# Decode attention and gated MLP in one kernel: q projection for both batch rows at once, turn sums on VectorE, the last part of W_up loaded apart, output in four column tiles

## The chip, the cores and the metric

One core of one Trainium2 chip. Times are device microseconds (us) of one execution, medians of several. The profile's span leaves out about 1.8 us that the measured time includes (661.62 us measured, span 659.8 us in the profiled run of before).

## The reference

Two batch rows, one new token each. A layer norm, attention over a cache of 8192 positions with 32 heads of 128, an output projection with residual, then a second layer norm and a gated MLP with residual. Everything is bf16.

```python
# B=2, Sq=1, D=512, 32 heads, Sk=8192, Dh=128, F=1376
xn = layernorm(x)
q = (xn @ wq) -> (B, 32, 1, 128)
p = softmax(q @ k_cache^T * 128**-0.5)          # k_cache, v_cache: (2, 32, 8192, 128)
h = x + (p @ v_cache) @ wo
g = layernorm(h) @ W_gate; u = layernorm(h) @ W_up
out = h + (relu(g) * u) @ W_down
```

The two caches hold 2 x 2 x 32 x 8192 x 128 x 2 bytes = 268 MB; with the weights, 281 MB have to be read.

## The kernel before

The heads are taken in 16 groups: 4 heads of one batch row each, 8.4 MB of K and 8.4 MB of V per group. K is multiplied by q and added up on VectorE, the exponential is taken on ScalarE, and V is weighted on TensorE. SBUF holds two K tiles and one V tile, so the loads form one long queue on SyncE.

```python
# q, before: one batch row at a time, 32 columns, 64 matmuls
for b in range(B):
    for g in range(0, NQ, QP):
        qps = ps_mm.tile([P, QP, Dh], f32, tag="mm", name="qps")
        for h in range(G):
            for c in range(KC):
                nc.tensor.matmul(out=qps[h*Q:(h+1)*Q], lhsT=xnb[:, c, b, :],
                                 rhs=wq_v[:, c, g:g+QP, h, :], ...)
        nc.scalar.activation(out=qrep[:, b, g:g+QP, :], in_=qps, func=ACT.Copy)
...
def blocks_of(o):            # four "turns" of o, scaled apart on ScalarE, summed by four matmuls
    osb = opool.tile([P, TG, Dh], f32, tag="row", name="osb")
    for t in range(TG):
        nc.scalar.activation(out=osb[:, t, :], in_=o[:, t*Dh:(t+1)*Dh], func=ACT.Copy,
                             scale=turn_of[:, t:t+1])
    return osb
...
for n in range(N - 1):
    scores(n, ...)           # VectorE, then ScalarE's exponentials
    load_k(n + 2)
    weighted_v(n)            # TensorE; at the end of a pair of groups: blocks_of and matmuls
    load_v(n + 1)
...
# the order of the last loads: wo, V of group 15 in four cuts, W_gate, W_up, W_down (three blocks
# and a remainder wd_l)
def y_rows(lhsT, rhs, first=False, last=False):
    m = lhsT.shape[1]
    for e in range(2):       # the output's two halves side by side in two column tiles of TensorE
        nc.tensor.matmul(out=y_ps[e*Q:e*Q+m], lhsT=lhsT, rhs=rhs[:, e*HD:(e+1)*HD], ...)
...
y_row = opool.tile([2 * Q, HD], bf16, tag="row")
nc.vector.tensor_copy(y_row, y_ps[0:2 * Q])
for e, eng in ((0, nc.sync), (1, nc.scalar)):
    eng.dma_start(out=out.rearrange("b s (h n) -> h (b s) n", n=HD)[e],
                  in_=y_row[e * Q:e * Q + B, :])
```

Here P = 128, Q = 32, KC = 4, HD = 256, B = 2. Each row of `o` counts in only one of its four blocks of 128 columns, its "turn"; the mask `turn_of` (0 or 1) picks that block. A column tile is a group of 32 output partitions that has matmuls of its own.

The softmax here doesn't subtract the row's maximum and nothing guards it: scores larger than these inputs give would overflow.

## Time and profile before

Median 661.66 us of three runs (661.63 to 661.9).

| | us | share of the span |
|---|---|---|
| VectorE busy | 592.1 | 90% |
| TensorE busy | 126.5 | 19% |
| ScalarE busy | 64.0 | 10% |
| packets on the load queue, as share of 16 engines | | 98.8% |

The page's busy line, its DMA line by slices of a 40th of the span, the table of DMA queues, and the shares of the chain that ended last, of the kernel before:

```profile
PE 126.5 (19%) x1390; PEld 64.0 (10%) x1391; DVE 592.1 (90%) x180; ACT 64.0 (10%) x175; POOL 2.5 (0%) x8
DMA  9999999999999999999999999999999999999996
q1 hardware_dynamic: 7124, 281.06, 98.8%
q8 instruction: 11, 0.18, 0.1%
DMA 77%; PE 15%; another core or an unknown queue 8%; issue 0%; DVE 0%; ACT 0%; ACTq 0%
```

VectorE's 90% looks like the limit, but the DMA engines are fuller: nine tenths or more in every slice but the last. The windows view of before shows it by stage; its last two columns are the DMA share and GB/s:

```profile
12.00:652.00 640.00, 120.83 (x1316) 59.73 (x1316) 587.30 (x150) 60.74 (x170) 0.00 (x0) 0.59 1.00 432
652.00:654.00 2.00, 1.52 (x43) 1.53 (x44) 0.05 (x1) 0.00 (x0) 0.00 (x0) 0.50 0.65 233
654.00:656.00 2.00, 1.67 (x20) 1.00 (x19) 0.24 (x2) 0.00 (x0) 0.00 (x0) 0.50 0.09 33
```

So for 640 us nothing is to be won unless fewer bytes are moved or the loads themselves run faster than this, and the end consists of what has to follow the stream. That end, from the timeline of before (start, duration, engine, line, operation, tiles):

```profile
652.48 1.74 PE L505 MATMUL up_ps<-hd,W 128*128 128x2 bf16 x44 [1.11 <-DMA W<-in_B_W_up_dram]
654.26 0.24 DVE L523 TENSOR_TENSOR act<-gate,up_ps 96x2 bf16<-96x2 f32 x2 [2.22 <-PE up_ps L505]
654.55 2.30 PE L456 MATMUL y_ps<-W,act 128*2 128x256 bf16 x20 [0.33 <-DVE act L523]
656.64 0.42 PE L456 MATMUL y_ps<-wd_l,act 96*2 96x256 bf16 x2
657.11 0.42 DVE L530 CAST y_row<-y_ps 64x256 bf16<-64x256 f32 x1 [2.61 <-PE y_ps L456]
657.55 0.32 SPq L532 DMA_DIRECT2D out_dram<-y_row  x1
657.55 0.26 ACTq L532 DMA_DIRECT2D out_dram<-y_row  x1
```

W_up's landing releases the up matmuls, they release the activation, that the y matmuls, then the cast and the two stores, issued at 657.55; the span ends 2.3 us later.

### The profile page before, as it was taken

The numbers are of one execution on the slowest core, as the hardware profiler recorded it, in microseconds if no ns is written. First come the engines' busy times: TensorE is split into PE (matmuls) and PEld (weight loads), VectorE is DVE, ScalarE is ACT, GpSimd is POOL, SyncE is SP. The second block draws the span as 40 slices with busy tenths as digits, with TensorE's granted clock in tenths as the row PEclk, the third lists the DMA queues.
The fourth block names the chain that finished last, engine by engine and source line by source line (L and its number), as shares of the span: only waits on it lengthen the run. The fifth ranks groups of instructions, "written<-read, shape, count | busy, mean of one in ns | idle before, by whom it ended". The sixth has DMA issues, their size and how long they took to land.

```text
span 659.8 us, 3322 instructions
## 1 busy us (share of the span) xinstructions
PE 126.5 (19%) x1390; PEld 64.0 (10%) x1391; DVE 592.1 (90%) x180; ACT 64.0 (10%) x175; POOL 2.5 (0%) x8
## 2 busy tenths in 40 slices
PE   2100302103030210404013030401203030030456
PEld 1000101001010000202002010100001010010225
DVE  2699999999998989989899998989899898999942
ACT  2101010010101010010102001010000101011020
POOL 1000000000000000000000000000000000000000
PEclk9755755757575565755656575565657555575766
DMA  9999999999999999999999999999999999999996
GB/s 382 445 445 445 402 425 441 445 445 434 402 441 437 445 434 413 433 437 438 441 433 418 441 425 445 434 429 429 425 441 438 441 421 437 421 442 437 402 413 248
DMA packets 7156, 281.28 MB, mean 426 GB/s; under 512 B 762, under 2 KB 1380, under 8 KB 2148
## 3 DMA queue, kind: packets, MB, share of 16 engines
q1 hardware_dynamic: 7124, 281.06, 98.8%
q8 instruction: 11, 0.18, 0.1%
q14 instruction: 5, 0.04, 0.0%
q10 hardware_dynamic: 16, 0.01, 0.0%
HBM read 281.06 MB, written 0.00 MB: 426 GB/s over the span
## 4 chain that ended last, share of the span: by engine, by line
DMA 77%; PE 15%; another core or an unknown queue 8%; issue 0%; DVE 0%; ACT 0%; ACTq 0%
DMA v<-in_A_v_cache_dram 70%; PE o L250 13%; DMA W<-in_B_W_up_dram 4%; DMA wq_sb<-in_A_wq_dram 2%; DMA W<-in_A_x_dram 1%; PE qps L175 1%; PE y_ps L456 0%; PE up_ps L505 0%; DVE y_row L530 0%; DVE act L523 0%; ACT osb L260 0%; ACTq L260 0%
## 5 line engine op out<-in xcount | busy, mean ns | idle before, releaser
L215 DVE TENSOR_TENSOR k<-k,qrep 128x32768 bf16<-128x32768 bf16 (+1 forms) x17 | 275.7, 16218 | 33.1 <-DMA k<-in_A_k_cache_dram 33.1
L221 DVE TENSOR_TENSOR k<-k 128x16384 bf16<-128x16384 bf16 (+3 forms) x68 | 266.8, 3923 | 2.3
L250 PE MATMUL o<-v,pm 128*32 128x512 bf16 x1016 | 90.9, 535 | 500.1 <-DMA v<-in_A_v_cache_dram 500.1
L250 PEld LDWEIGHTS <-pm 128*32 128x32 bf16 x1016 | 38.6, 129 | 550.3 <-issue 381.7
L227 ACT ACTIVATE pm<-sc 32x256 bf16<-32x256 f32 x64 | 47.2, 737 | 346.6 <-DVE sc L224 345.3
L224 DVE TENSOR_REDUCE sc<-k 128x256 f32<-128x2048 bf16 (+1 forms) x17 | 36.7, 2160 | 2.0 <-DVE k L221 0.5
L260 ACT ACTIVATE osb<-o,turn_of 128x128 f32<-128x128 f32 x36 | 10.3, 368 | 210.5 <-PE o L250 210.5
L227 ACT ACTIVATION_READ_ACCUMULATOR pm<-sc 32x1 f32 x64 | 15.0, 234 | 0.0
L296 PE MATMUL rep<-osb,spread 128*64 128x128 f32 (+1 forms) x64 | 9.9, 297 | 3.9 <-ACT osb L260 3.9
L462 DVE TENSOR_SCALAR o_sum<-o,turn_of 128x128 f32<-128x128 f32 x1 | 0.3, 350 | 10.8 <-PE o L250 10.8
L296 PEld LDWEIGHTS rep<-osb,spread 128*64 128x64 f32 (+1 forms) x64 | 7.3, 161 | 8.7 <-ACT osb L260 7.8
L175 PE MATMUL qps<-wq_sb,xnb 128*32 128x512 bf16 x64 | 5.7, 532 | 4.8 <-DMA wq_sb<-in_A_wq_dram 4.8
L442 PE MATMUL ar_ps<-W,oc 128*2 128x512 bf16 x28 | 3.2, 626 | 11.4 <-DVE oc L347 11.4
L152 DVE COPY xc<-x_ps 128x8 f32<-128x8 f32 x1 | 0.2, 167 | 4.9 <-PE x_ps L149 4.9
L505 PEld LDWEIGHTS <-W 128*128 128x128 bf16 (+1 forms) x88 | 3.4, 122 | 1.4 <-DMA W<-in_B_W_up_dram 1.2
L175 PEld LDWEIGHTS <-xnb 128*32 128x32 bf16 x64 | 2.8, 123 | 7.3 <-issue 5.8
L181 ACT ACTIVATE qrep<-qps 128x512 bf16<-128x512 f32 x4 | 2.4, 597 | 6.5 <-PE qps L175 6.5
L530 DVE CAST y_row<-y_ps 64x256 bf16<-64x256 f32 x1 | 0.4, 417 | 2.6 <-PE y_ps L456 2.6
L456 PE MATMUL y_ps<-W,act 128*2 128x256 bf16 x20 | 2.3, 415 | 0.3 <-DVE act L523 0.3
L523 DVE TENSOR_TENSOR act<-gate,up_ps 96x2 bf16<-96x2 f32 (+1 forms) x2 | 0.2, 160 | 2.2 <-PE up_ps L505 2.2
L320 PE MATMUL zb<-zm,same 128*128 128x4 f32 (+2 forms) x12 | 2.0, 283 | 0.3 <-ACT ol_f L287 0.3
L442 PEld LDWEIGHTS <-oc 128*2 128x2 bf16 x28 | 0.8, 113 | 12.9 <-DVE oc L347 11.5
(91 smaller groups left out, 47.6 us busy)
## 6 DMA issues: line engine op xcount, KB each, us to landing
k<-in_A_k_cache_dram SPq DMA_DIRECT2D x2, 4096.0 KB, 30.8
wq_sb<-in_A_wq_dram SPq DMA_DIRECT2D x1, 4096.0 KB, 12.3
v<-in_A_v_cache_dram SPq DMA_DIRECT2D x1, 4096.0 KB, 15.8
v<-in_A_v_cache_dram SPq DMA_DIRECT2D x1, 3072.0 KB, 22.8
W<-in_A_wo_dram SPq DMA_DIRECT2D x1, 2048.0 KB
W<-in_B_W_gate_dram SPq DMA_DIRECT2D x1, 1376.0 KB, 26.9
W<-in_B_W_up_dram SPq DMA_DIRECT2D x1, 1376.0 KB
W<-in_A_wo_dram SPq DMA_DIRECT2D x1, 1024.0 KB, 28.7
```

Of the source, the lines that this page charges most:

```text
L175: nc.tensor.matmul(out=qps[h * Q:(h + 1) * Q], lhsT=xnb[:, c, b, :], rhs=wq_v[:, c, g:g + QP, h, :], start=(c == 0), stop=(c == KC - 1),)
L181: nc.scalar.activation(out=qrep[:, b, g:g + QP, :], in_=qps, func=ACT.Copy)
L215: nc.vector.tensor_tensor(out=kp, in0=kp, in1=_view(qrep[:, b, i, :], 0, [[0, hi - lo], [1, Dh]]), op=ALU.mult)
L221: nc.vector.tensor_tensor(out=kp[:, :, 0:half], in0=kp[:, :, 0:half], in1=kp[:, :, half:width], op=ALU.add)
L224: nc.vector.tensor_reduce(out=sc[:, lo:hi], in_=kp[:, :, 0:8], axis=AXIS.X, op=ALU.add)
L227: nc.scalar.activation(out=p_of[ps, :, :, h], in_=sc[ps, :].rearrange("p (g t) -> p g t", t=TG), func=ACT.Exp, accum_out=(zm[ps, b, i:i + ...
L250: nc.tensor.matmul(out=o[g:g + W2], lhsT=_view(pm, (0 if lane else R) + t // TG * W2, [[1, W2]]), rhs=vt[:, t:t + TG, :].rearrange("p t d ...
L260: nc.scalar.activation(out=osb[:, t, :], in_=o[:, t * Dh:(t + 1) * Dh], func=ACT.Copy, scale=turn_of[:, t:t + 1])
L296: nc.tensor.matmul(out=reps[where][at:at + m, max(k - 1, 0), :], lhsT=spread[n_of].rearrange("k u h m -> k (u h m)"), rhs=osb[:, t, :], st ...
L442: nc.tensor.matmul(out=ar_ps[g:g + B], lhsT=oc[:, k, :], rhs=wo_sb[:, k, :], start=False, stop=(k + P // Q >= NK), skip_group_check=True)
L456: nc.tensor.matmul(out=y_ps[e * Q:e * Q + m], lhsT=lhsT, rhs=rhs[:, e * HD:(e + 1) * HD], start=first, stop=last, skip_group_check=True)
L505: nc.tensor.matmul(out=ps[0:w, fc, :], lhsT=lhsT, rhs=hd[:, c, :], start=(c == 0 and fc == 0), stop=(c == KC - 1), skip_group_check=True)
```

## The change

Its intent: halve the matmuls of the q projection; replace four scalings and four f32 matmuls per pair of groups by four VectorE operations and one matmul, and do them after the next scores; let most of the up matmuls start before the last quarter of W_up; run the y matmuls four at a time. The diff, cut to its core:

```diff
-    for b in range(B):
-        for g in range(0, NQ, QP):
+    for g in range(0, NQ, QP):
+        for h0 in range(0, G, 2):
             qps = ps_mm.tile([P, QP, Dh], f32, tag="mm", name="qps")
...             (lhsT now holds both rows: 64 columns, 32 matmuls)
-            nc.scalar.activation(out=qrep[:, b, g:g + QP, :], in_=qps, func=ACT.Copy)
+            for b in range(B):
+                for h in range(2):
...                 (src, dst: 32 partitions each)
+                    if h == 0:
+                        nc.scalar.activation(out=dst, in_=src, func=ACT.Copy)
+                    else:
+                        nc.vector.tensor_copy(dst, src)
-    def blocks_of(o):
...
+    def lanes_of(o):
+        osb = opool.tile([P, Dh], f32, tag="row", name="osb")
+        nc.vector.tensor_scalar_mul(osb, o[:, 0:Dh], turn_of[:, 0:1])
+        for t in range(1, TG):
+            nc.vector.scalar_tensor_tensor(out=osb, in0=o[:, t * Dh:(t + 1) * Dh],
+                                           scalar=turn_of[:, t:t + 1], in1=osb,
+                                           op0=ALU.mult, op1=ALU.add)
         return osb
...     for n in range(N - 1):  scores(n); load_k(n + 2);
+        collect()           # lanes_of and one matmul, for the pair that ended with group n - 1
...     weighted_v(n); load_v(n + 1)
-    for g, w in ((0, B_W_gate), (1, B_W_up)):
+    for g, w, c0, c1 in ((0, B_W_gate, 0, KC), (1, B_W_up, 0, KC - 1), (1, B_W_up, KC - 1, KC)):
...
     scores(N - 1)
+    collect()
...     def y_rows
-        for e in range(2):
-            nc.tensor.matmul(out=y_ps[e * Q:e * Q + m], lhsT=lhsT, rhs=rhs[:, e * HD:(e + 1) * HD],
+        for c in range(KC):
+            nc.tensor.matmul(out=y_ps[c * Q:c * Q + m], lhsT=lhsT, rhs=rhs[:, c * P:(c + 1) * P],
...     (the residual row is loaded as 8 rows of 128 to match)
-    y_row = opool.tile([2 * Q, HD], bf16, tag="row")
-    nc.vector.tensor_copy(y_row, y_ps[0:2 * Q])
-    for e, eng in ((0, nc.sync), (1, nc.scalar)):
-        eng.dma_start(out=out.rearrange("b s (h n) -> h (b s) n", n=HD)[e],
-                      in_=y_row[e * Q:e * Q + B, :])
+    y_row = opool.tile([P, P], bf16, tag="row")
+    nc.vector.tensor_copy(y_row, y_ps)
+    for b, eng in ((0, nc.sync), (1, nc.scalar)):
+        eng.dma_start(out=out[b].rearrange("s (c n) -> (s c) n", n=P),
+                      in_=y_row.rearrange("(c q) n -> q c n", q=Q)[b])
```

More of the change, by code (lines that the diff above doesn't have):

```diff
@@ L169 @@
     wq_v = wq_sb.rearrange("p c (i h d) -> p c i h d", h=G, d=Dh)
-    for b in range(B):
-        for g in range(0, NQ, QP):
+    for g in range(0, NQ, QP):
+        for h0 in range(0, G, 2):
             qps = ps_mm.tile([P, QP, Dh], f32, tag="mm", name="qps")
-            for h in range(G):
+            for h in range(2):
                 for c in range(KC):
                     nc.tensor.matmul(
-                        out=qps[h * Q:(h + 1) * Q],
-                        lhsT=xnb[:, c, b, :],
-                        rhs=wq_v[:, c, g:g + QP, h, :],
+                        out=qps[h * B * Q:(h + 1) * B * Q],
+                        lhsT=xnb[:, c].rearrange("p b q -> p (b q)"),
+                        rhs=wq_v[:, c, g:g + QP, h0 + h, :],
                         start=(c == 0), stop=(c == KC - 1),
                     )
-            nc.scalar.activation(out=qrep[:, b, g:g + QP, :], in_=qps, func=ACT.Copy)
+            for b in range(B):
+                for h in range(2):
+                    src = qps[(h * B + b) * Q:(h * B + b + 1) * Q]
+                    dst = qrep[(h0 + h) * Q:(h0 + h + 1) * Q, b, g:g + QP, :]
+                    if h == 0:
+                        nc.scalar.activation(out=dst, in_=src, func=ACT.Copy)
+                    else:
+                        nc.vector.tensor_copy(dst, src)
     seq = [(b, i) for b in range(B) for i in range(NQ)]
@@ L254, in v_moving @@
                              stop=(last and t + P // Q * TG >= hi), skip_group_check=True)
-    def blocks_of(o):
-        osb = opool.tile([P, TG, Dh], f32, tag="row", name="osb")
-        for t in range(TG):
-            nc.scalar.activation(out=osb[:, t, :], in_=o[:, t * Dh:(t + 1) * Dh], func=ACT.Copy,
-                                 scale=turn_of[:, t:t + 1])
+    def lanes_of(o):
[5 more added lines that the diff above has]
+                                           op0=ALU.mult, op1=ALU.add)
         return osb
@@ L277, in weighted_v, with collect @@
         v_moving(n, o, 0, T, lane, first=(lane == 0), last=done)
-        if not done:
+        pair["done"] = (o, b, i) if done else None
+    def collect():
+        if not pair.get("done"):
             return
-        osb = blocks_of(o)
+        o, b, i = pair.pop("done")
+        osb = lanes_of(o)
         if i == LQ:
             o_l = ps_s.tile([P, G], f32, tag="st", name="o_l")
-            for t in range(TG):
-                nc.tensor.matmul(out=o_l, lhsT=osb[:, t, :], rhs=lane_of[:, 0, :],
-                                 start=(t == 0), stop=(t == TG - 1))
-            ol_f = misc.tile([P, G], f32)
-            nc.scalar.activation(out=ol_f, in_=o_l, func=ACT.Copy)
-            return ol_f
+            nc.tensor.matmul(out=o_l, lhsT=osb, rhs=lane_of[:, 0, :], start=True, stop=True)
+            nc.vector.tensor_copy(ol_f, o_l)
+            return
+        k, u = place(i)
         where = 0 if k == 0 else 1
@@ L294, in weighted_v @@
         m = min(n_of, 2) * (P // n_of)
-        for t in range(TG):
-            nc.tensor.matmul(out=reps[where][at:at + m, max(k - 1, 0), :],
-                             lhsT=spread[n_of].rearrange("k u h m -> k (u h m)"),
-                             rhs=osb[:, t, :], start=(t == 0), stop=(t == TG - 1),
-                             skip_group_check=True)
+        nc.tensor.matmul(out=reps[where][at:at + m, max(k - 1, 0), :],
+                         lhsT=spread[n_of].rearrange("k u h m -> k (u h m)"),
+                         rhs=osb, start=True, stop=True, skip_group_check=True)
     def gather(k):
@@ L366 @@
     between = {5: lambda: gather(0), NQ + 1: first_row, NQ + 5: lambda: gather(0)}
+    ol_f = misc.tile([P, G], f32)
     HALVES = (0, T // 2, T)
@@ L372 @@
     for n in range(N - 1):
-        if n in between:
-            between[n]()
         scores(n, HALVES if n == 0 else (0, T))
@@ L377 @@
             load_k(n + 2)
-        ret = weighted_v(n)
+        collect()
+        if n == NQ:
+            z0 = z_tile()
+            zb0, zl0 = row_z(0, z0[:, 0:LQ]), last_z(0, z0[:, LQ:])
+        if n in between:
+            between[n]()
+        weighted_v(n)
         if n + 2 < N:
             load_v(n + 1)
-        if n == NQ - 1:
-            ol_f = ret
-            z0 = z_tile()
-            zb0, zl0 = row_z(0, z0[:, 0:LQ]), last_z(0, z0[:, LQ:])
     W = kring.tile([P, RING], bf16, tag="k", name="W")
@@ L395 @@
     at += NF * D
-    HD = D // 2
-    x_q = W[0:2 * B, at:at + HD]
+    x_q = W[0:KC * B, at:at + P]
     for k, n in enumerate(SIZES):
@@ L405 @@
     load_v(N - 1, CUTS)
-    nc.scalar.dma_start(out=x_q, in_=A_x.rearrange("b s (h n) -> (b s h) n", n=HD))
-    for g, w in ((0, B_W_gate), (1, B_W_up)):
-        nc.sync.dma_start(out=wgu[:, g].rearrange("p c n -> p (c n)"),
-                          in_=w.rearrange("(p c) n -> p (c n)", c=KC))
+    nc.scalar.dma_start(out=x_q, in_=A_x.rearrange("b s (h n) -> (b s h) n", n=P))
+    for g, w, c0, c1 in ((0, B_W_gate, 0, KC), (1, B_W_up, 0, KC - 1), (1, B_W_up, KC - 1, KC)):
+        nc.sync.dma_start(out=wgu[:, g, c0:c1].rearrange("p c n -> p (c n)"),
+                          in_=w.rearrange("(p c) n -> p (c n)", c=KC)[:, c0 * F:c1 * F])
     blocks = [(f, min(4, NF - f)) for f in range(0, NF, 4)]
@@ L450 @@
                          start=(c == 0), stop=False, skip_group_check=True)
-    y_ps = ps_mm.tile([P, HD], f32, tag="mm")
+    y_ps = ps_mm.tile([P, P], f32, tag="mm")
     def y_rows(lhsT, rhs, first=False, last=False):
         m = lhsT.shape[1]
-        for e in range(2):
-            nc.tensor.matmul(out=y_ps[e * Q:e * Q + m], lhsT=lhsT, rhs=rhs[:, e * HD:(e + 1) * HD],
+        for c in range(KC):
+            nc.tensor.matmul(out=y_ps[c * Q:c * Q + m], lhsT=lhsT, rhs=rhs[:, c * P:(c + 1) * P],
                              start=first, stop=last, skip_group_check=True)
@@ L460 @@
     v_moving(N - 1, o15, CUTS[1], CUTS[2], first=False)
-    o_sum = opool.tile([P, Dh], f32, tag="row", name="o_sum")
-    nc.vector.tensor_scalar_mul(o_sum, o15[:, 0:Dh], turn_of[:, 0:1])
-    for t in range(1, TG):
-        nc.vector.scalar_tensor_tensor(out=o_sum, in0=o15[:, t * Dh:(t + 1) * Dh],
-                                       scalar=turn_of[:, t:t + 1], in1=o_sum,
-                                       op0=ALU.mult, op1=ALU.add)
+    o_sum = lanes_of(o15)
     zlb = last_z(L, z_tile()[:, 0:G])
-    for e in range(2):
-        nc.tensor.matmul(out=y_ps[e * Q:e * Q + B], lhsT=ident[0:2 * B, e:2 * B:2], rhs=x_q,
+    for c in range(KC):
+        nc.tensor.matmul(out=y_ps[c * Q:c * Q + B], lhsT=ident[0:KC * B, c:KC * B:KC], rhs=x_q,
                          start=False, stop=False, skip_group_check=True)
```

## The prediction

> **What bounds the kernel now.** The stream of loads. The queue table gives 281.06 MB on the one load queue, filling 98.8% of 16 engines' span. The windows give a DMA share of 1.00 and 432 GB/s from 12 to 652 us, then 0.65 (652-654) and 0.09 (654-656). The chain of waits is 70% "v from the V cache"; its matmuls (13%) hide a K load already queued. VectorE is busy 90% but follows: it idles 33.1 us in all for K loads, 1.9 to 2.4 us per group in the timeline. The change removes no bytes, so only the few us after the stream can shrink.
>
> **Loop.** Four scalings of o on ScalarE (368 ns each, 9 times) become four operations on VectorE. The last group already does exactly that: 0.35 + 1.12 = 1.47 us. Nine times is 13 us more for VectorE, 1.47 us in a group, under its idling. K loads are issued before the new work; one at 322 us is issued 21 us before its predecessor in the queue (V) has landed. So the queue never runs dry: worth 0. Four f32 spreading matmuls become one, also hidden.
>
> **Head.** The q projection falls from 64 matmuls in 5.71 us to 32 in about 2.9. VectorE cannot start before the first half of K lands at 22.86 us, and q is ready at 19.5 now: worth 0. Sixteen partial copies replace four, done by about 20 us.
>
> **Tail.** Before: W_up lands 652.4, up matmuls to 654.2 (44 in 1.74 us), y 654.55 to 657.07, cast 0.42, store issued 657.55, end 659.8.
> - W_up's last quarter apart: three quarters of the up matmuls could run earlier, gaining up to 1.3 us. But the collect of group 14 now follows the last scores (631.7): 1.47 us plus a matmul of about 0.5 go ahead of the attention row projection. The second V part has landed by 643.2, so about 1.1 us of that reaches the gate matmuls, which then end near 652, not 651. The slack there (PE waits 1.1 us for W_up) is used up; up matmuls should end 654.0 to 654.4, a gain near 0.
> - The remainder of W_down, issued at 643.26, takes 12.6 us: it lands at 655.9 and holds the last y matmuls.
> - y: two 256-column matmuls run together at about 230 ns a pair. Four of 128 columns halve the streaming, but the up matmuls show 39 ns issue each, so about 160 ns for four: 11 x 160 = 1.7 us instead of 2.5. Gain 0.8. The Trainium skill, "TensorE: Matmul & The Clock Gate" (Part 3), says thin matmuls in different column groups run concurrently; the 8 ol matmuls in 0.60 us (272 ns each) agree.
> - cast of 128 rather than 256 columns: 0.42 to about 0.25.
> - store and residual: 256-byte rows instead of 512. The skill, "DMA: Bandwidth & Descriptors" (Specifications), says under 512 B a read-modify-write happens. No run here shows it; I allow 0.1 us.
> - The residual row is issued earlier, ending SyncE's 3.8 us wait for it before W_up. The queue is full then: 0.
>
> Sum: about -0.9 us. Predicted 660.7 us, 8 in 10 within 659.7 to 661.8. Chances: faster by over 2% 0.005, within 2% 0.985, slower 0.01.
>
> **What would show it.** DMA share still 1.00 and 432 GB/s to 652 us; VectorE's idling for K about 13 us smaller in all, ScalarE's busy time about 10 us lower; attention row projection starting near 636, not 633.8; y matmuls in 1.7 us ending near 656.3; cast near 0.25.
>
> **What would make it wrong.** VectorE falling behind so that K loads are issued late (DMA share dips; several us slower). The stream's rate moving by itself: 0.3% is 2 us. The collect in the tail costing more than its slack, or nothing, shifting the end by 1 us.

## The result, and the profile after

661.18 us median of six runs (661.03 to 661.44), against 661.64 us (661.54 to 661.9, six runs) before: 0.46 us less. Ratio 0.9992, 95% interval 0.998 to 1.0005: the same. The interval includes no change. Ratios here are of fast runs of the same rounds, and not quite the ratio of the medians quoted.

The same lines of the page, of the changed kernel:

```profile
PE 119.5 (18%) x1341; PEld 58.6 (9%) x1341; DVE 609.6 (92%) x225; ACT 55.8 (8%) x142; POOL 2.5 (0%) x8
DMA  9999999999999999999999999999999999999996
q1 hardware_dynamic: 7272, 281.06, 98.9%
q8 instruction: 10, 0.16, 0.1%
DVE 62%; DMA 33%; PE 3%; issue 1%; ACT 0%; DVEq 0%
```

The chain turned from 77% DMA to 62% VectorE, though hardly a microsecond changed. Following back who released whom leads through VectorE whenever it, and not a transfer, was the last to be ready at a step; it does not say that a faster VectorE would end the kernel sooner. The windows of the changed kernel decide that:

```profile
12.00:652.00 640.00, 114.36 (x1244) 54.18 (x1243) 604.38 (x191) 52.61 (x137) 0.00 (x0) 0.58 1.00 432
652.00:654.00 2.00, 2.00 (x47) 1.97 (x46) 0.57 (x4) 0.00 (x0) 0.00 (x0) 0.50 0.70 243
654.00:656.00 2.00, 1.66 (x45) 1.07 (x44) 0.24 (x2) 0.00 (x0) 0.00 (x0) 0.50 0.05 17
```

Still 1.00 and 432 GB/s until 652 us. The end, from the timeline of the changed kernel:

```profile
652.34 1.72 PE L510 MATMUL up_ps<-hd,W 128*128 128x2 bf16 x44
654.09 0.24 DVE L528 TENSOR_TENSOR act<-gate,up_ps 96x2 bf16<-96x2 f32 x2 [0.94 <-PE up_ps L510]
654.38 1.55 PE L466 MATMUL y_ps<-W,act 128*2 128x128 bf16 x40 [0.33 <-DVE act L528]
655.76 0.28 PE L466 MATMUL y_ps<-wd_l,act 96*2 96x128 bf16 x4
656.09 0.29 DVE L535 CAST y_row<-y_ps 128x128 bf16<-128x128 f32 x1 [1.76 <-PE y_ps L466]
656.41 0.65 SPq L537 DMA_DIRECT2D out_dram<-y_row  x1
656.41 0.62 ACTq L537 DMA_DIRECT2D out_dram<-y_row  x1
```

The stores are issued at 656.41, 1.14 us earlier. But the span ends at 659.43 instead of 659.84: issue to end takes 3.02 us instead of 2.29. So 0.73 us of a gain of 1.14 is given back by the store (1.14 less the 0.41 by which the span is shorter). Over all traces here, issue to end takes 2.94 to 3.02 us with this store (the changed kernel, s4, s7 to s10) and 2.29 to 2.38 us with two stores out of neighbouring partitions (before, s1, s6): 0.56 to 0.73 us more. Issuing itself takes 0.65 and 0.62 us instead of 0.32 and 0.26.

The head changed, too. In the changed kernel the partial copies of q on ScalarE and VectorE alternate, each waiting for the other, until 24.46 us:

```profile
15.04 0.59 ACT L186 ACTIVATE qrep<-qps 32x512 bf16<-32x512 f32 x1 [4.49 <-PE qps L175]
15.66 0.69 DVE L188 CAST qrep<-qps 32x512 bf16<-32x512 f32 x1 [3.89 <-ACT qrep L186]
16.38 1.20 ACT L186 ACTIVATE qrep<-qps 32x512 bf16<-32x512 f32 x2 [0.75 <-DVE qrep L188]
...
23.76 0.70 DVE L188 CAST qrep<-qps 32x512 bf16<-32x512 f32 x1 [0.65 <-ACT qrep L186]
24.49 8.69 DVE L222 TENSOR_TENSOR k<-k,qrep 128x16384 bf16<-128x16384 bf16 x1
```

The scores start 1.6 us later than before, where VectorE waited for K until 22.86 us. The first line below is from the timeline of before; the others are from the waits views of before and of the changed kernel (total us, times, longest), and sum up all of VectorE's waits for K:

```profile
22.86 8.69 DVE L215 TENSOR_TENSOR k<-k,qrep 128x16384 bf16<-128x16384 bf16 x1 [11.06 <-DMA k<-in_A_k_cache_dram]
DVE k L215 <- DMA k<-in_A_k_cache_dram: 33.1, 11, 11.1
DVE k L222 <- DMA k<-in_A_k_cache_dram: 8.8, 7, 2.3
```

The alternation comes from waits in the program as built. The kernel's text writes none, but in the trace each VectorE copy carries a wait for a semaphore that ScalarE's copies raise, and every second ScalarE copy carries one for a semaphore that VectorE's raise. Why these waits were put in, and whether the copies could overlap without them, no run here shows.

What do the y matmuls wait for? The timeline merges them. Single starts and landings, read from the trace of the changed kernel (us):

```
load            median of its 16 landings   last landing   first y matmuls that need it
W_down block 0          651.66                 653.38          654.39 (when act is ready)
W_down block 1          653.02                 654.92          654.96
W_down block 2          653.71                 655.52          655.56
W_down remainder        654.06                 655.73          655.77
```

Three times TensorE starts 0.04 us after the last landing. So the four-tile y is no longer limited by its matmuls but by the loads again. The Trainium skill ("DMA: Bandwidth & Descriptors", Why a DMA increments its semaphore by 16 and not by 1) says that a DMA runs on up to 16 engines that finish independently, and that only the full count means all has landed. This trace agrees: 16 landings per load, the last 1.7 to 1.9 us after the median in this table.

### The profile page after: what moved, and what is told of

Read it like the earlier page. It is cut to its first block, busy times and chain, and to the rows that moved or that the text cites. A ratio compares the mean times of both kernels' runs of the same rounds, so it can differ in the third digit from the quotient of the medians.

```text
span 659.4 us, 3234 instructions
## 1 busy us (share of the span) xinstructions
PE 119.5 (18%) x1341; PEld 58.6 (9%) x1341; DVE 609.6 (92%) x225; ACT 55.8 (8%) x142; POOL 2.5 (0%) x8
## 4 chain that ended last, share of the span: by engine, by line
DVE 62%; DMA 33%; PE 3%; issue 1%; ACT 0%; DVEq 0%
DMA k<-in_A_k_cache_dram 31%; DVE k L222 29%; DVE k L228 28%; DVE sc L231 4%; DMA wq_sb<-in_A_wq_dram 2%; DVE osb L268 1%; DVE qrep L188 1%; PE qps L175 1%; PE o L257 1%; PE ar_ps L452 0%; ACT qrep L186 0%; PE y_ps L466 0%; PE a_ps L459 0%; PE gate_ps L510 0%; PE up_ps L510 0%
## 5 line engine op out<-in xcount | busy, mean ns | idle before, releaser
L257 PE MATMUL o<-v,pm 128*32 128x512 bf16 x1016 | 88.1, 522 | 395.8 <-DMA v<-in_A_v_cache_dram 395.8
L307 PE MATMUL rep<-osb,spread 128*64 128x128 f32 (+1 forms) x16 | 5.9, 474 | 110.5 <-DVE osb L268 110.5
L307 PEld LDWEIGHTS rep<-osb,spread 128*64 128x64 f32 (+1 forms) x16 | 3.2, 257 | 114.1 <-DVE osb L268 114.1
L188 DVE CAST qrep<-qps 32x512 bf16<-32x512 f32 x8 | 5.5, 692 | 7.2 <-ACT qrep L186 7.1
L266 DVE TENSOR_SCALAR osb<-o,turn_of 128x128 f32<-128x128 f32 x10 | 3.4, 344 | 9.2 <-PE o L257 9.2
L268 DVE SCALAR_TENSOR_TENSOR osb<-o,turn_of,osb 128x128 f32<-128x128 f32 x30 | 10.5, 351 | 1.1
L175 PE MATMUL qps<-wq_sb,xnb 128*64 128x512 bf16 x32 | 6.5, 562 | 7.0 <-DMA wq_sb<-in_A_wq_dram 4.8
L186 ACT ACTIVATE qrep<-qps 32x512 bf16<-32x512 f32 x8 | 4.7, 586 | 8.5 <-PE qps L175 5.2
L175 PEld LDWEIGHTS <-xnb 128*64 128x64 bf16 x32 | 2.7, 147 | 10.0 <-issue 5.3
L330 PEld LDWEIGHTS zb<-zm,same 128*128 128x128 f32 x12 | 2.1, 258 | 0.8 <-issue 0.4
```

The costliest lines, as they stand in the source:

```text
L175: nc.tensor.matmul(out=qps[h * B * Q:(h + 1) * B * Q], lhsT=xnb[:, c].rearrange("p b q -> p (b q)"), rhs=wq_v[:, c, g:g + QP, h0 + h, :], ...
L186: nc.scalar.activation(out=dst, in_=src, func=ACT.Copy)
L188: nc.vector.tensor_copy(dst, src)
L257: nc.tensor.matmul(out=o[g:g + W2], lhsT=_view(pm, (0 if lane else R) + t // TG * W2, [[1, W2]]), rhs=vt[:, t:t + TG, :].rearrange("p t d ...
L268: nc.vector.scalar_tensor_tensor(out=osb, in0=o[:, t * Dh:(t + 1) * Dh], scalar=turn_of[:, t:t + 1], in1=osb, op0=ALU.mult, op1=ALU.add)
L307: nc.tensor.matmul(out=reps[where][at:at + m, max(k - 1, 0), :], lhsT=spread[n_of].rearrange("k u h m -> k (u h m)"), rhs=osb, start=True, ...
```

## The experiments

Each batch of four shared nine runs of the kernel before on the same chip; the four kernels of a batch ran five times each. All results were correct.

### Which property of the store costs the time?

**s1: before, with rows of 256 B out of neighbouring partitions.** The cast leaves a gap between the halves of a row, so the two cannot go as one piece.

```diff
-    y_row = opool.tile([2 * Q, HD], bf16, tag="row")
-    nc.vector.tensor_copy(y_row, y_ps[0:2 * Q])
+    y_row = opool.tile([2 * Q, 2, HD], bf16, tag="row")
+    nc.vector.tensor_copy(y_row[:, :, 0:P], y_ps[0:2 * Q].rearrange("p (h n) -> p h n", n=P))
...
+        eng.dma_start(out=out.rearrange("b s (e h n) -> e (b s) h n", e=2, n=P)[e],
+                      in_=y_row[e * Q:e * Q + B, :, 0:P])
```

> The kernel before, whose cast leaves a gap between the two halves of a row, so that each of the two store DMAs moves 4 rows of 256 B out of 2 neighbouring partitions instead of 2 rows of 512 B. In the trace of before, issue of a store took 0.32 us (SyncE) and 0.26 us (ScalarE), and 2.3 us passed from store issue to the end of the span; in the changed kernel 0.65 and 0.62 us, and 3.0 us. Theory A (size or number of rows sets the cost): issue near 0.6 us, about 3.0 us from issue to end, whole kernel about 0.7 us slower than before (about 662.3 us). Theory B (the spread of the rows over partitions 32 apart sets it): issue 0.3 us, 2.3 us to the end, same time as before within 0.2 us.

Measured: 661.89 us median (before 661.7 in the same rounds), ratio 0.9999 (0.9987 to 1.0012). Its packets are of 256 B in the trace, four per store. Timeline of s1:

```profile
657.79 0.32 SPq L532 DMA_DIRECT2D out_dram<-y_row  x1
657.79 0.27 ACTq L532 DMA_DIRECT2D out_dram<-y_row  x1
```

The span ends at 660.10, 2.31 us after issue. Neither the size of the rows nor their number costs anything that this trace shows (2.29 us from issue to end in before): theory A falls.

**s2: before, with rows of 512 B out of partitions 32 apart.**

```diff
-    for e, eng in ((0, nc.sync), (1, nc.scalar)):
-        eng.dma_start(out=out.rearrange("b s (h n) -> h (b s) n", n=HD)[e],
-                      in_=y_row[e * Q:e * Q + B, :])
+    for b, eng in ((0, nc.sync), (1, nc.scalar)):
+        eng.dma_start(out=out[b].rearrange("s (e n) -> (s e) n", n=HD),
+                      in_=y_row.rearrange("(e q) n -> q e n", q=Q)[b])
```

> The kernel before, each store DMA now takes one batch row: 2 rows of 512 B out of partitions 32 apart, as the changed kernel picks its rows. Theory A (size or number of rows): no change, issue 0.3 us, 2.3 us from issue to end, same time as before within 0.2 us. Theory B (spread over partitions): issue near 0.6 us, 3.0 us to the end, about 0.7 us slower than before.

Measured: 662.49 us median, ratio 1.0013 (0.9999 to 1.0027), mean 0.8 us over that of before. Timeline of s2:

```profile
657.83 0.63 SPq L532 DMA_DIRECT2D out_dram<-y_row  x1
657.84 0.60 ACTq L532 DMA_DIRECT2D out_dram<-y_row  x1
```

The span ends at 660.70, 2.87 us after issue. Two rows of 512 B cost nearly what the four rows of 256 B of the changed kernel cost (2.94 to 3.02 us), once they are picked 32 partitions apart. Theory B holds against theory A: it is which rows a store takes, not their size or number. But the two ends of the store changed together. In every run, a store out of partitions 32 apart also writes 1 KB of the output in one piece, and a store out of neighbouring partitions writes pieces of both batch rows. No run parts these, so that it is the step in SBUF, and not the order in the output, is not shown. The first store's packets start 1.2 us after the start of its issue instead of 0.8 us in s1, the other's 1.5 instead of 0.8.

**s3: the changed kernel with four stores of two neighbouring partitions each.**

```diff
-    for b, eng in ((0, nc.sync), (1, nc.scalar)):
-        eng.dma_start(out=out[b].rearrange("s (c n) -> (s c) n", n=P),
-                      in_=y_row.rearrange("(c q) n -> q c n", q=Q)[b])
+    for c in range(KC):
+        (nc.sync, nc.scalar)[c % 2].dma_start(
+            out=out.rearrange("b s (c n) -> c (b s) n", n=P)[c],
+            in_=y_row[c * Q:c * Q + B, :])
```

> The changed kernel with four store DMAs of 2 rows of 256 B from neighbouring partitions, two on each issuing engine, instead of two of 4 rows. Under theory A with the number of rows as the cause each issue takes about 0.3 us and the two on one engine 0.6 in sum: no gain, within 0.2 us of the changed kernel (661.2 us). With the size of the rows as the cause each issue takes about 0.6 us and the two 1.2: 0.5 us slower than the changed kernel. Under theory B (spread) each takes 0.3 us, the first lands early, the second 0.3 us later: about 0.3 us faster than the changed kernel.

Measured: 660.88 us median (660.71 to 661.27), ratio to before 0.9987 (0.9975 to 1.0). Timeline of s3:

```profile
656.40 0.61 SPq L537 DMA_DIRECT2D out_dram<-y_row  x2
656.41 0.58 ACTq L537 DMA_DIRECT2D out_dram<-y_row  x2
```

Each engine issues two stores in the time that one took, and the span ends at 659.00 us, 2.60 us after issue, 0.43 us sooner than in the changed kernel. This is the version that came out fastest. Its 0.3 us over the changed kernel come from different rounds; in its own rounds s4, which stores as the changed kernel does and issues at 656.38 us, took 661.32 us. The traces, with the stores issued at the same time, are the better evidence.

One DMA for all eight rows could not be tried: by the author's account, a view that steps the partitions in two dimensions was refused before any run, and the record has nothing of it. (The Trainium skill, "DMA: Bandwidth & Descriptors", Rules for kernel authors, says that the partition is taken from the first dimension alone; no run here shows it.) So whether one store on one engine would do better is left open.

### What do the other parts bring?

**s4: the changed kernel with the loop's turn sums on ScalarE again,** in the order of before; the last group stays.

```diff
-        osb = lanes_of(o)
+        osb = blocks_of(o)          # as in the kernel before, with its four matmuls
...     in the loop
-        collect()
...
         weighted_v(n)
         load_v(n + 1)
+        collect()
...
     scores(N - 1)
-    collect()
```

> The changed kernel with the turn sums of the loop on ScalarE again (four scalings, four matmuls, before the next scores), the last group as in both kernels. Theory C (the last matmuls wait for the last W_down loads, which land at 655.5 and 655.7 us in the trace, not for the work before them): the attention row projection starts near 634 us rather than 636.4, the gate matmuls about 1 us earlier, but the y matmuls still end near 656.0 and the time stays within 0.2 us of the changed kernel (661.2 us). Rival D (as the prediction had it: the collect after the last scores costs about 1.1 us in the tail and cancels the split of W_up): the end comes about 1 us earlier, near 660.2 us. VectorE's idling for K loads grows from 8.9 to about 22 us under both.

Measured: 661.32 us median (661.11 to 661.45), ratio to before 0.9993 (0.998 to 1.0005). VectorE's idling for K loads is 20.6 us, as expected, and the attention row projection (the matmuls into ar_ps) starts at 633.69 us instead of 636.38. Timeline of s4:

```profile
653.02 0.24 DVE L539 TENSOR_TENSOR act<-gate,up_ps 96x2 bf16<-96x2 f32 x2 [1.09 <-PE up_ps L521]
653.50 0.60 PE L477 MATMUL y_ps<-W,act 128*2 128x128 bf16 x16 [0.52 <-DMA W<-in_B_W_down_dram]
654.89 1.01 PE L477 MATMUL y_ps<-W,act 128*2 128x128 bf16 x24 [0.79 <-DMA W<-in_B_W_down_dram]
655.71 0.30 PE L477 MATMUL y_ps<-wd_l,act 96*2 96x128 bf16 x4
656.38 0.66 SPq L548 DMA_DIRECT2D out_dram<-y_row  x1
```

The activation is ready at 653.3 us, 1.1 us earlier, and the y matmuls now name the W_down loads as what they wait for. The stores are issued at 656.38 instead of 656.41. Theory C holds, rival D falls: the collect after the last scores takes 2.7 us from the attention row projection and nothing from the kernel, because the last landing comes later than all of it.

**s5: before with the y part alone,** and the store of s3. (Edit: the y and residual lines of the change's diff, and the store of s3's.)

> The kernel before with only the y part of the change (four column tiles of 128, residual as 8 rows) and the store as four DMAs of two neighbouring partitions. Theory C (after the tiling the end is set by the last W_down landing, in the traces 655.7 to 656.0 us, plus 0.3 us of matmuls, 0.3 us of cast and 2.6 us of this store): it ends as run s3 does, near 660.9 us, 0.7 us faster than before; q projection, turn sums and W_up split add nothing. Rival E (the other parts bring some of the gain): it is 0.3 us or more slower than s3.

Measured: 661.0 us median (660.81 to 661.21), ratio to before 0.9989 (0.9976 to 1.0002); span 659.09 against 659.00 of s3. Its y matmuls run from 654.30 to 656.07, its stores are issued at 656.43. The y part alone brings all that s3 brings, within what can be told here.

**s6: the changed kernel with y in two tiles,** and the residual and store of before.

> The changed kernel with y in two tiles of 256 and the residual and store of before. y at 0.21 us a pair from 654.4: y matmuls end near 656.9, cast 0.42, store 2.3 us: end of span near 659.7, about 661.5 us measured, 0.3 us slower than the changed kernel and within 0.2 us of before. Under rival E it keeps a gain of 0.3 us or more over before.

Measured: 662.43 us median, but in two groups (661.24 and 661.33; 662.43 to 662.72), ratio to before 1.0008 (0.9994 to 1.0021). The expected 661.5 us was met by the first group and missed by 0.9 us by the median; why there are two groups is not known. By time this is inconclusive at the level of tenths; it shows no gain over before. In its trace y ran from 653.84, waited 0.18 us for W_down at 655.03, and ended at 656.69, 0.2 us earlier than I expected; the stores were issued at 657.17 and the span ended at 659.55.

**s7: the changed kernel with W_up in one load.**

```diff
-    for g, w, c0, c1 in ((0, B_W_gate, 0, KC), (1, B_W_up, 0, KC - 1), (1, B_W_up, KC - 1, KC)):
+    for g, w, c0, c1 in ((0, B_W_gate, 0, KC), (1, B_W_up, 0, KC)):
```

> The changed kernel with W_up in one load. In its trace W_up's two parts had landed at 651.2 and 652.0 us and the up matmuls began at 652.3, after the variance matmul, so the split was used by nothing: same time as the changed kernel (661.2 us) within 0.2 us. Rival E: slower by up to 1.3 us.

Measured: 661.54 us median (661.22 to 661.75), ratio to before 0.9996 (0.9983 to 1.0008). Its own trace ran 0.6 us late in the gate matmuls, so W_up, landed at 652.43, was again waited for by nobody (up matmuls from 652.97). The time is 0.36 us over that of the changed kernel, of other rounds, and so misses the 0.2 us expected; this run alone does not settle what the split is worth to some tenths. s5 is the better evidence: with W_up in one load it ends as s3 does, with the split. By this delay the trace answers another question, since each block of W_down had now landed before its turn came (block 1 at 655.11 for a start at 655.40, block 2 at 655.73 for 655.83, the remainder at 655.93 for 656.04). Timeline of s7:

```profile
655.02 1.24 PE L466 MATMUL y_ps<-W,act 128*2 128x128 bf16 x40 [0.33 <-DVE act L528]
656.04 0.32 PE L466 MATMUL y_ps<-wd_l,act 96*2 96x128 bf16 x4
```

From the start of the first chunk (655.02) to that of the eleventh (656.04) pass 1.02 us: 0.10 us for the four matmuls of a chunk.

**s8: the changed kernel with the q projection of before.** (Edit: the first block of the change's diff undone.)

> The changed kernel with the q projection of before. Scores start near 22.9 us again instead of 24.5, because the partial copies of the changed kernel alternate between ScalarE and VectorE until 24.5; VectorE's idling for K loads grows, and the time is the same as the changed kernel's (661.2 us) within 0.2 us, since the stream of loads is full meanwhile. A rival that the late start costs its 1.6 us would show 659.6 us.

Measured: 661.37 us median (661.27 to 661.8), ratio to before 0.9996 (0.9983 to 1.0008). The scores start at 22.80 us, and VectorE idles 21.6 us for K loads instead of 8.8, 11.3 us of it in front of the first load. Neither the halved projection nor the later start of the scores shows in the time: the queue was full meanwhile.

### Why does the last landing lag?

The lag of the last of 16 landings behind the median went from 0.2 us early in the kernel to 1.7 to 1.9 us at its end, in steps, and shrank slowly between some of them. The table of DMA queues has two queues marked "instruction"; one of them, q8, moved 10 packets of 16 KB in the changed kernel: at 77.5 us, then about every 78 us, and at 618.4, 644.5 and 653.5 us. Each took 1.0 to 1.1 us there. The first step of the lag (0.22 to 1.28 us) lies between the loads that landed at 71 and 92 us.

**s9 and s10: the changed kernel with 64 and with 128 dummy matmuls** before the q projection, one look each.

```diff
+    pad = ps_mm.tile([P, 2], f32, tag="mm", name="pad")
+    for _ in range(64):          # s10: 128
+        nc.tensor.matmul(out=pad, lhsT=_view(zero, 0, [[0, P]]), rhs=_view(zero, 0, [[0, 2]]),
+                         start=True, stop=True)
```

> The changed kernel with 64 dummy matmuls (128 instructions on TensorE) before the q projection, where TensorE waits for weights. In the traces, the queue marked instruction moves 16 KB at a time for TensorE, at 618.4, 644.5 and 653.5 us in the changed kernel, and the last of 16 landings of a load lags their median by 0.8 us before 644.5 and by 1.6 us after it. Theory F (each such fetch takes one load engine's time, and the load on that engine then lands late): the fetches of the tail come 128 instructions earlier, the middle one near 640 us, and the step of the lag from 0.8 to 1.6 us moves with it, so loads landing at 641 to 644 lag by 1.6 us already. Rival G (the lag grows where the weights' smaller rows begin): the step stays after 644.5. The time stays within 0.4 us of the changed kernel under both.

> The same with 128 dummy matmuls (256 instructions, 16 KB if one is 64 B as 16 KB per fetch and the spacing of the fetches suggest): one more fetch early on, the fetches of the tail where they were (618.4, 644.5, 653.5 us within 0.5 us), and the step of the lag again between the loads landing at 644.5 and at 648.7 us.

Measured: 661.19 us both, one run each, so of unknown state (before 661.43 on the same chip). From the three traces:

```
kernel    instruction packets of 16 KB near the end   lag (us) by the load's last landing
changed   618.4  644.5  653.5                         0.78 at 644.5   1.63 at 648.7
s9        641.0  650.3  654.5                         0.81 at 634.8   1.79 at 643.1
s10       618.7  644.6  653.5                         0.57 at 614.6   1.85 at 620.8
```

In s9 the middle packet came 3.6 us earlier and the step moved in front of the load that landed at 643.1: rival G falls. In s10 there is one packet more in all (11 instead of 10) and those of the tail came back to their old places, as expected, which shows that they carry TensorE's instructions (256 per 16 KB, so 64 B each). But there the step came with the packet at 618.7, not with that at 644.6: the expected place of the step was missed. The first step of the kernel moved, too. The first packet came at 17.2 us in s9 and at 13.6 us in s10, instead of 77.5, and in both the lag was already 1.5 us for the load that landed at 24.0 us, where the changed kernel reached 1.28 us only at 92. So here a step of the lag followed such a packet, but not each packet raises the largest lag, and which one does is not settled; the trace does not say which of the 16 engines a packet used. The last landing was at 655.7 us in all three, so this set the place of the lag, not the time.

## Why the prediction was right or wrong

The total was right: 660.7 us predicted, 661.18 measured, within 659.7 to 661.8, and within 2% of before. That alone says little, since the range of 2.1 us also holds the time of before. Its largest claim, that the stream of loads leaves only the last few us, held: 1.00 and 432 GB/s to 652 us in both traces. The gain was half of what was expected, 0.46 instead of 0.9 us, and the interval of the ratio does not exclude none at all. Point by point:

- **Store: the step that failed, a term mis-sized.** The prediction allowed 0.1 us for "256-byte rows instead of 512". It cost 0.73 us in this pair of traces, and not for that reason: 256 B rows cost nothing in s1, and 512 B rows cost nearly the same as in the changed kernel in s2. What costs it is that a store takes its rows 32 partitions apart, for one whole batch row, instead of from neighbouring partitions; which end of the transfer matters stays open. The skill's remark on transfers under 512 B ("DMA: Bandwidth & Descriptors", Specifications) was the wrong thing to look at for rows this few.
- **y matmuls: right size, wrong reason.** 1.7 us predicted from "160 ns for four"; 1.66 us measured. But four matmuls start every 0.10 us where nothing holds them (s7), and the rest is waiting for W_down. The concurrency taken from the skill ("TensorE: Matmul & The Clock Gate", Part 3) agrees with s7: ten chunks of four 128-column matmuls started within 1.02 us, where the two-tile kernel took 0.21 us a chunk.
- **W_up apart: right that it gains near 0, incomplete in why.** The up matmuls ended at 654.06, inside the 654.0 to 654.4 given. The prediction blamed the collect of group 14; s4 removes it, makes the activation 1.1 us earlier, and gains nothing. The last landing of W_down, which the prediction named in its own line as holding the last y matmuls, is the limit in both cases.
- **Attention row projection near 636:** 636.38. **Cast about 0.25:** 0.29.
- **Loop worth 0:** shown by s4 (and s5). VectorE's idling for K fell by 24 us (33.1 to 8.8), not 13. The missing 11 us are the first wait of the kernel, which the copies of q now fill (s8: 11.3 us of 21.6 are back).
- **Head worth 0:** right (s8), but the copies were done at 24.5 us, not "by about 20": the two engines do not copy at the same time; they alternate, by waits in the built program.
- **ScalarE about 10 us less busy:** 8.2 us less (64.0 to 55.8), since the q copies added some.

## What to carry to other kernels

When a stream of loads fills the queue to the end, ask of every speed-up in the tail what lands last; work ahead of the last landing is free, and only what follows it counts. Look at the store as a part of that tail: how its rows are picked can give back most of what the matmul arrangement that led to it gains (here 0.73 of 1.14 us). A chain of waits that changes its colour, as here from 77% DMA to 62% VectorE, is no finding by itself; the busy share by stage is.

## What the Trainium skill lacked or had wrong

- "DMA: Bandwidth & Descriptors" gives a 512 B minimum and has no word on what these runs show: a store whose rows lie 32 partitions apart (and next to one another in the output) took 0.60 to 0.66 us to issue, against 0.25 to 0.32 us from neighbouring partitions, whatever the row size, and ended the kernel about 0.6 us later (s1 against s2: 2.31 and 2.87 us from issue to end).
- The same page gives its 512 B minimum for line rate. For eight rows of 256 B no cost of it is visible: 2.31 us from issue to end in s1, 2.29 in before.
- "Runtime: NRT & Kernel Launch" (Instruction fetch mechanics) says that instructions are fetched in blocks of 16 KiB, 256 at a time, as s10 shows here. I found no page that says what such a fetch costs a full stream of loads: 10 or 11 packets of 16 KB on one queue in these kernels took 0.9 to 1.3 us each, and the lag of a load's last landing rises in steps after some of them (s9, s10), to 1.9 us.
